# A list schedule that also counts the transfers: softcap attention and a bilinear layer on one core

## The chip, the core and the metric

One core of a Trainium2 chip runs the whole kernel. A time is what one execution takes on the device, in microseconds (us). Of the kernel before there are three runs and one execution with a profile.

## The reference

For 4 batches and 12 heads of 448 rows by 64 columns, in fp32:

```
scores = (q @ k.T) / sqrt(64)
scores = cap * tanh(scores / cap)
attn   = softmax(scores)
x      = attn @ v                        # 1792 x 768 after the heads are put side by side
out    = ((x @ w_a) * (x @ w_b)) @ w_out # 768 -> 1536 -> 768
```

The three weights arrive as float64, so each weight tile is twice as large in DRAM as the fp32 tile that is made of it.

## The kernel before, in words

Attention works on 24 pairs of heads. The first 12 pairs (two batches) are worked through alone. Then the bilinear layer for these two batches (group 0) is interleaved with the attention of pairs 12 to 23, and the layer for group 1 ends the program. TensorE's order is written out by hand (`chain`), and it stays as it is.

A pair goes so. K and Q come in transposed blocks by transfers of their own (`load_k`, four for K and four for Q, two pairs at a time in pairs 2 to 11), and VectorE transposes them (`turn`, tk and tq). TensorE makes the scores of four key blocks (psc), ScalarE takes tanh and exp (pf), VectorE adds up for the row sums (psum), TensorE multiplies with V (`attend`, tile pv, L308) and gathers the sums (L329). Then comes the division: `recip` on VectorE (rec), `store_rec` to DRAM (rd), `load_den` back as a broadcast (den), `scale` on VectorE (L358), and `split_x` into a high and a low part (xhi, xlo). In pairs 0 to 10 the pv bank is `pi % 4`, and pair 11 has bank 0: so the attend of pair 4 waits for the scale of pair 0, and that of pair 11 for the scale of pair 8.

A weight comes in 36 tiles ("units": a0, b0, a1, b1, ... of w_a and w_b, then those of w_out). A raw unit (w64, two transfers of 384 KB, `load64`) is turned into fp32 in six steps on ScalarE, VectorE and GpSimd (`conv`), and then split in two (wha and wla, ...). In group 0 the raw units of the first six come over GpSimd's queue, which also brings V of pairs 3 to 11 (`load_v`); nearly all the other transfers are issued by SyncE (SP). Each queue issues in order, and one that waits holds up all behind it.

Every piece of work is a `job` with an engine, a guessed duration, a lag and what it needs. Due times are worked out backwards from the hand-written chain; then a list schedule walks forward in a modelled time and gives each engine, of the jobs that are ready, the one that is due first. In that model a transfer has only a fixed lag (the last numbers of `job`), however many others are under way. The first four raw units may start from a modelled time of `RAW + 4.0 * (2 * t + n)` on.

Of the kernel before, what the change touches and what calls it, by code (L numbers as in the profile page):

```python
# [119 lines left out]
def kernel(  # L120
# [12 lines left out]
    B, H, S, D = q.shape  # L133
    NT, DM = out.shape
    DFF = w_a.shape[1]
    P = 128
    NP = H // 2
    NK = DM // P
# [57 lines left out]
    own, krem = (slice(0, D), slice(D, P)), (S - R, 0)  # L196
    raw, stk, prob, pvs = {}, {}, {}, {}
# [184 lines left out]
    seq = [(nm, f, g) for g in range(NG) for nm, f in one]  # L382
    wraw, wfull, wspl = {}, {}, {}

    def load64(t, n):
        nm, f, _ = seq[t]
        w = {"a": w_a, "b": w_b, "o": w_out}[nm].bitcast(I32)
        if n == 0:
            wraw[t] = wp.tile([P, DM, 2], I32, tag="w64", name=f"w64{nm}_{f}", bufs=2)
        rt = wraw[t]  # L390
        eng = nc.gpsimd if t < 6 else nc.sync
        if nm == "o":
            eng.dma_start(rt[own[n]].rearrange("p n t -> p (n t)"), w[f * P + n * D : f * P + (n + 1) * D, :])
        else:
            eng.dma_start(
                rt[own[n]].rearrange("p (k f) t -> p k (f t)", k=NK),
                w.rearrange("(j k p) f -> j p k f", j=2, p=D)[n][:, :, 2 * f * P : 2 * (f + 1) * P],
            )

    def conv(t, step):  # L400
# [118 lines left out]
    def job(key, eng, us, fn, args, needs=(), lag=None, after=0.0):  # L519
        jobs[key] = Piece(eng, us, LAG[eng] if lag is None else lag, list(needs), fn, args, after)  # L520
# [133 lines left out]

    used = {"n": 0}
    CYCLE, turns_of = ((0, 1, 2), (3, 1, 2, 0)), [3, 3, 1, 2, None]
    SOON, RAW = 4.0, 18.0
    HASTY = (gate, keep_a, collect, recip, store_rec, load_den, scale)
    GAP = 20.4

# [39 lines left out]
    for r in range(NPG):  # L700
        h = r // NP
        free = [(kind, pi, hf) for kind in ("attend", "add") for pi in (NPAIR - 2, NPAIR - 1) for hf in range(2)]
# [6 lines left out]
    ring = {"o": [], "ab": []}  # L709
    for t, (nm, f, g) in enumerate(seq):  # L710
        if g == 0:
            for n in range(2):
                needs = [("raw", t, 0)] if n else [("conv", t - 2, 5)]
                job(("raw", t, n), "POOL" if t < 6 else "SP", 0.8 if t < 6 else 0.5, load64, (t, n), needs, 6.0, RAW + 4.0 * (2 * t + n) if t < 4 else 0.0)
                jobs["raw", t, n].order_only = n > 0
            steps = (("ACT", 0.82), ("ACT", 0.8), ("DVE", 0.48), ("DVE", 0.48), ("DVE", 0.88), ("POOL", 2.1))
            for n, (eng, us) in enumerate(steps):
                needs = [("raw", t, 0), ("raw", t, 1)] if n == 0 else [("conv", t, n - 1)]
                if n == 1:
                    needs += [("lo", t - AHEAD), ("keepw", t - AHEAD), ("full", t - 1)]  # L720
                job(("conv", t, n), eng, us, conv, (t, n), needs, 2.0 if t < 5 else 0.5)
            job(("keepw", t), "SP", 0.52, store_w, (t,), [("conv", t, 5)], 3.0)
            jobs["full", t] = jobs["conv", t, 1]
            made = ("conv", t, 5)
        else:
            job(("full", t), "SP", 0.5, reload_w, (t,), [("lo", t - AHEAD), ("keepw", t - AHEAD), ("full", t - 1), ("keepw", t - NW)])
            made = ("full", t)
        before = ring["o" if nm == "o" else "ab"]
        free = [("hi", before[-1])] if before else []
        if len(before) >= 3:  # L730
            free.append(used[seq[before[-3]]])
        before.append(t)
        on_dve = g and nm == "b"
        job(("hi", t), "DVE" if on_dve else "ACT", 0.5 if on_dve else 0.74, split_hi, (t,), [made, *free])
        job(("lo", t), "DVE", 0.88, split_lo, (t,), [("hi", t)])
        jobs["w", nm, g, f] = jobs["lo", t]
# [63 lines left out]
    free = dict.fromkeys(LAG, 0.0)  # L800
    line = [jobs[k] for k in chain]
    wait = {e: [] for e in LAG}
    for x in real:
        x.left = len(x.from_)
        x.ready = x.after
        if not x.left and x.eng != "PE":
            wait[x.eng].append(x)
    order, port = [], 0.0
    for x in real:
        x.shared = x.eng == "DVE" and x.fn not in (turn, recip, scale, collect) and not (x.fn is gate and x.args[3] == 0)  # L810
    while len(order) < len(real):
        best = None
        for e, xs_ in wait.items():
            if e == "PE":
                xs_ = line[:1] if line and not line[0].left else []
            if xs_:
                t = max(free[e], min(max(x.ready, port if x.shared else 0.0) for x in xs_))
                if best is None or t < best[0]:
                    best = (t, e, xs_)
        t, e, xs_ = best  # L820
        x = min((x for x in xs_ if max(x.ready, port if x.shared else 0.0) <= t), key=lambda x: x.due - (SOON if x.fn in HASTY else 0.0))
        (line if e == "PE" else wait[e]).remove(x)
        x.start, x.end = t, t + x.us + x.lag
        free[e] = t + x.us
        if x.fn is conv and e == "POOL":
            port = t + x.us
        order.append(x)
        for y in x.then:
            y.left -= 1
            y.ready = max(y.ready, t + x.us if y.order_only and y.eng == x.eng else x.end - y.early.get(id(x), 0.0))  # L830
            if not y.left and y.eng != "PE":
                wait[y.eng].append(y)
# [45 lines left out]
```

## Time and profile before

| | us |
|---|---|
| three runs | 732.89, 737.08, 737.47; median 737.08 |
| the profiled execution | 735.1 |
| its span (first to last instruction) | 733.2 |
| TensorE busy in the span | 706.3 (96%) |
| VectorE, ScalarE, GpSimd busy | 420.9, 349.8, 105.0 |
| mean granted TensorE clock | 0.99 |

The profiled execution is 1.9 us longer than its span. TensorE is the engine that is nearly always busy; the others have long pauses. A row's number in brackets at its end is the idle time of the engine ahead of that instruction and what released it. SPq is SyncE's queue of transfers: there the duration of a row is how long the issue took.

### The profile page before, as it was taken

Reading aid. Unit: us, or ns where it says so; the run is one execution under the profiler, and the core shown is the slowest. Engines: PE = TensorE matmul, PEld = TensorE weight load, DVE = VectorE, ACT = ScalarE, POOL = GpSimd, SP = SyncE. Lnnn points to the kernel's source line nnn. Section 1 sums busy time; section 2 is a strip of 40 time slices with the busy share of each in tenths; the row PEclk is TensorE's granted clock in tenths of the full one; section 3 lists DMA queues with packets and bytes.
Section 4 is the critical chain, followed back from the end, with each engine's and each line's share of the span. In section 5 each row is a group of like instructions: output and inputs, shape, how many; then the busy total and the mean of one; then the engine's idle time right before and its main releaser. Section 6 shows DMA issues by size and latency. Waiting matters only on the chain.

```text
span 733.2 us, 11184 instructions
## 1 busy us (share of the span) xinstructions
PE 706.3 (96%) x4370; PEld 578.8 (79%) x4370; DVE 420.9 (57%) x649; ACT 349.8 (48%) x474; POOL 105.0 (14%) x88
## 2 busy tenths in 40 slices
PE   7868999899999999999999999999999999999996
PEld 2323336598898798798798798999999999999996
DVE  3447996766747868777896847543033434343322
ACT  6875996476776774586655640122322102202100
POOL 0514541122222222222222200000000000000000
PEclk9988999999999999999999999999999999999999
DMA  9988456677777576666575536431022103101012
GB/s 129 185 121 171 128 142 151 151 181 165 168 210 158 139 206 154 148 177 173 149 186 145 156 112 216 155 108 47 19 69 83 43 22 108 44 22 44 1 44 110
DMA packets 142482, 90.54 MB, mean 123 GB/s; under 512 B 107768, under 2 KB 128280, under 8 KB 142424
## 3 DMA queue, kind: packets, MB, share of 16 engines
q1 hardware_dynamic: 135784, 82.53, 45.3%
q0 software_dynamic: 2784, 6.79, 4.0%
q10 hardware_dynamic: 3856, 0.46, 0.5%
q8 instruction: 36, 0.59, 0.4%
q14 instruction: 22, 0.18, 0.1%
HBM read 67.24 MB, written 22.50 MB: 122 GB/s over the span
## 4 chain that ended last, share of the span: by engine, by line
PE 84%; DMA 5%; SPq 4%; DVE 3%; issue 1%; ACT 1%; ACTq 0%; DVEq 0%
PE po L491 8%; PE phb L458 8%; PE po L493 8%; PE po L492 8%; PE phb L460 8%; PE phb L459 8%; PE pha L458 8%; PE pha L460 8%; PE pha L459 8%; PE pv L308 7%; PE psc L271 4%; SPq L220 3%; DMA acc<-in_q_dram 2%; DMA rd<-rec 2%; PE pv L329 1%
## 5 line engine op out<-in xcount | busy, mean ns | idle before, releaser
L491 PE MATMUL po<-who,gh 128*128 128x384 f32 x336 | 113.3, 337 | 0.0
L493 PE MATMUL po<-who,gl 128*128 128x384 f32 x336 | 112.3, 334 | 0.0
L492 PE MATMUL po<-wlo,gh 128*128 128x384 f32 x336 | 112.3, 334 | 0.0
L458 PE MATMUL pha<-xhi,wha 128*128 128x448 f32 x288 | 104.8, 364 | 3.3 <-DVE xhi L374 3.3
L458 PE MATMUL phb<-xhi,whb 128*128 128x448 f32 x288 | 105.1, 365 | 0.0
L460 PE MATMUL pha<-xhi,wla 128*128 128x448 f32 x288 | 104.8, 364 | 0.0
L459 PE MATMUL pha<-xlo,wha 128*128 128x448 f32 x288 | 104.5, 363 | 0.2 <-DVE xlo L375 0.2
L460 PE MATMUL phb<-xhi,wlb 128*128 128x448 f32 x288 | 104.5, 363 | 0.0
L459 PE MATMUL phb<-xlo,whb 128*128 128x448 f32 x288 | 104.2, 362 | 0.0
L283 ACT ACTIVATE pf<-psc,capt 128x896 f32<-128x896 f32 (+1 forms) x96 | 84.4, 910 | 38.9 <-PE psc L271 20.6
L308 PE MATMUL pv<-pf,vb 128*64 128x448 f32 x384 | 80.8, 564 | 8.9 <-DVE den L358 7.1
L287 ACT ACTIVATE pf<-pf,capt 128x1792 f32<-128x1792 f32 (+1 forms) x48 | 77.0, 1605 | 0.7
L502 DVE TENSOR_TENSOR acc<-po,acc 128x384 f32<-128x384 f32 x84 | 46.3, 554 | 44.8 <-PE po L493 44.7
L308 PEld LDWEIGHTS pv<-pf,vb 128*64 128x64 f32 x384 | 26.5, 142 | 56.5 <-issue 38.5
L465 ACT COPY asb<-pha 128x448 f32<-128x448 f32 x48 | 25.6, 533 | 94.0 <-PE pha L460 93.7
L475 DVE TENSOR_TENSOR asb<-phb,asb 128x448 f32<-128x448 f32 x48 | 29.9, 624 | 65.8 <-PE phb L460 65.6
L491 PEld LDWEIGHTS po<-who,gh 128*128 128x128 f32 x336 | 63.1, 188 | 2.7 <-issue 1.5
L492 PEld LDWEIGHTS po<-wlo,gh 128*128 128x128 f32 x336 | 63.1, 188 | 0.1
L493 PEld LDWEIGHTS po<-who,gl 128*128 128x128 f32 x336 | 63.1, 188 | 0.0
L458 PEld LDWEIGHTS pha<-xhi,wha 128*128 128x128 f32 x288 | 53.9, 187 | 9.4 <-DVE xhi L374 3.6
L477 ACT CAST gh<-asb 128x448 fp32r<-128x448 f32 x48 | 27.2, 567 | 67.3 <-DVE asb L475 66.9
L458 PEld LDWEIGHTS phb<-xhi,whb 128*128 128x128 f32 x288 | 53.9, 187 | 6.5 <-issue 2.5
(103 smaller groups left out, 1030.9 us busy)
## 6 DMA issues: line engine op xcount, KB each, us to landing
w64o<-in_moe_w_out_dram SPq DMA_DIRECT2D x24, 384.0 KB
w64a<-in_moe_w_a_dram SPq DMA_DIRECT2D x18, 384.0 KB
w64b<-in_moe_w_b_dram SPq DMA_DIRECT2D x18, 384.0 KB
den<-rd SPq DMA_DIRECT2D x48, 112.0 KB
out_dram<-acc SPq DMA_DIRECT2D x13, 384.0 KB
wda<-wta SPq DMA_DIRECT2D x12, 384.0 KB
wdb<-wtb SPq DMA_DIRECT2D x12, 384.0 KB
wdo<-wto SPq DMA_DIRECT2D x12, 384.0 KB
```

What stands on the lines that cost most here:

```text
L271: nc.tensor.matmul(psc[:, j, :S], kk, tq[y][o], start=(x + y == 0), stop=(x == 1))
L283: nc.scalar.activation(to, prob.pop((pi, "s", c))[:, :n, :S], AF.Tanh, scale=capt[:, 1:2])
L287: nc.scalar.activation(pf, pf, AF.Exp, scale=capt[:, 0:1])
L308: nc.tensor.matmul(t[o, :S], tv[:, j * (NC3 + 1) + (c if j == 0 else (c + 1) % (NC3 + 1))], p, start=(c == 0), stop=(c == NC3))
L458: nc.tensor.matmul(t[:, :S], wh[:, kk], xhi[:, kk, cs], start=(kk == 0), stop=False)
L459: nc.tensor.matmul(t[:, :S], wh[:, kk], xlo[:, kk, cs], start=False, stop=False)
L460: nc.tensor.matmul(t[:, :S], wl[:, kk], xhi[:, kk, cs], start=False, stop=(kk == NK - 1))
L475: nc.vector.tensor_mul(t, phs.pop(("b", h))[:, :S], t)
L491: nc.tensor.matmul(t[:, :HALF], gh[:, cs], wh, start=(f == fs[0]), stop=False)
L492: nc.tensor.matmul(t[:, :HALF], gh[:, cs], wl, start=False, stop=False)
L493: nc.tensor.matmul(t[:, :HALF], gl[:, cs], wh, start=False, stop=(f == fs[-1]))
L502: nc.vector.tensor_add(acc[:, ti, hs], t, acc[:, ti, hs])
```

## The change

The model gets a server for transfers. `MOVE` gives each transfer a duration; `moved` is the time at which the server will have done all that was issued; a transfer that is not `store_rec` or `load_den` may not be issued while more than `BACKLOG` = 3 us are outstanding, and its end is reckoned from the server. `RAW` goes from 18 to 24, the first four raw units come in six transfers each of 128 KB (`parts`), with other earliest times, and the lag behind the conversion steps of the first units is 0.5 where it was 2.0. No arithmetic changes. The order of TensorE's instructions is the same as before; those of the other engines move.

```diff
-    def load64(t, n):
+    def load64(t, n, parts):
...
-        rt = wraw[t]
+        j, i = n % 2, n // 2
+        rt = wraw[t][own[j]]
...
+            ks = slice(2 * i * NK // parts, 2 * (i + 1) * NK // parts)
             eng.dma_start(
-                rt[own[n]].rearrange("p (k f) t -> p k (f t)", k=NK),
-                w.rearrange("(j k p) f -> j p k f", j=2, p=D)[n][:, :, 2 * f * P : 2 * (f + 1) * P],
+                rt.rearrange("p (k f) t -> p k (f t)", k=NK)[:, ks],
+                w.rearrange("(j k p) f -> j p k f", j=2, p=D)[j][:, ks, 2 * f * P : 2 * (f + 1) * P],
             )
...
-    SOON, RAW = 4.0, 18.0
+    SOON, RAW, BACKLOG = 4.0, 24.0, 3.0
...
-            for n in range(2):
-                needs = [("raw", t, 0)] if n else [("conv", t - 2, 5)]
-                job(("raw", t, n), "POOL" if t < 6 else "SP", 0.8 if t < 6 else 0.5, load64, (t, n), needs, 6.0, RAW + 4.0 * (2 * t + n) if t < 4 else 0.0)
+            parts = 6 if t < 4 else 2
+            for n in range(parts):
+                needs = [("raw", t, n - 1)] if n else [("conv", t - 2, 5)]
+                job(("raw", t, n), "POOL" if t < 6 else "SP", 0.8 if t < 6 else 0.5, load64, (t, n, parts), needs, 4.0, RAW + 6.0 * (t + n / parts) if t < 4 else 0.0)
...
-                job(("conv", t, n), eng, us, conv, (t, n), needs, 2.0 if t < 5 else 0.5)
+                job(("conv", t, n), eng, us, conv, (t, n), needs, 0.5)
...
-    order, port = [], 0.0
+    order, port, moved = [], 0.0, 0.0
+    MOVE = {load_k: 0.46, load_v: 0.5, load64: 1.7, store_rec: 0.15, load_den: 0.4, store_w: 1.0, reload_w: 1.0, store_x: 0.57, reload_x: 0.65, store_out: 1.0}
+    def starts(x):
+        t = x.ready
+        if x.shared:
+            t = max(t, port)
+        if x.move and x.fn not in (store_rec, load_den):
+            t = max(t, moved - BACKLOG)
+        return t
...
-                t = max(free[e], min(max(x.ready, port if x.shared else 0.0) for x in xs_))
+                t = max(free[e], min(starts(x) for x in xs_))
...
+        if x.move:
+            moved = max(moved, t + 1.3) + x.move
+            x.end = max(x.end, moved + 0.7)
```

GpSimd's queue in the first 12 pairs, before. vb_175, vb_176 and vb_177 are the three buffers of V; the first two rows bring V of pair 3, which may start once the attend of pair 0 is done, and so on.

```order
L230 DMA vb_175<-in_v_dram 128x3x64 x2
L232 DMA vb_175<-in_v_dram 64x64 x2
L395 DMA w64a_337<-in_moe_w_a_dram 64x6x256 x2
L230 DMA vb_176<-in_v_dram 128x3x64 x2
L232 DMA vb_176<-in_v_dram 64x64 x2
L395 DMA w64b_405<-in_moe_w_b_dram 64x6x256 x2
L230 DMA vb_177<-in_v_dram 128x3x64 x2
L232 DMA vb_177<-in_v_dram 64x64 x2
```

The same queue in the changed kernel:

```order
L230 DMA vb_175<-in_v_dram 128x3x64 x2
L232 DMA vb_175<-in_v_dram 64x64 x2
L230 DMA vb_176<-in_v_dram 128x3x64 x2
L232 DMA vb_176<-in_v_dram 64x64 x2
L397 DMA w64a_402<-in_moe_w_a_dram 64x2x256 x2
L230 DMA vb_177<-in_v_dram 128x3x64 x2
L232 DMA vb_177<-in_v_dram 64x64 x2
L397 DMA w64a_402<-in_moe_w_a_dram 64x2x256 x2
```

Ahead of V of pair 5 (the first vb_177) stood two whole raw units, 1,536 KB; now two pieces of one, 256 KB. The second unit starts four loads of V later.

SP's queue around the first reciprocals, before. rec_403 are those of pair 0, rd_93 is where they go in DRAM, den_433 what comes back.

```order
L220 DMA acc<-in_k_dram 32x28x32
L220 DMA acc<-in_q_dram 32x28x32
L341 DMA rd_93<-rec_403 7x2x64
L351 DMA den_433<-rd_93 64x448 x2
L220 DMA acc<-in_k_dram 32x28x32 x2
L220 DMA acc<-in_q_dram 32x28x32
L341 DMA rd_94<-rec_470 7x2x64
```

The same place in the changed kernel (rec_378 is the former rec_403):

```order
L220 DMA acc<-in_k_dram 32x28x32
L858 TENSOR_LOAD bounded
L858 ISA x2
L341 DMA rd_93<-rec_378 7x2x64
L220 DMA acc<-in_q_dram 32x28x32
L220 DMA acc<-in_k_dram 32x28x32
L220 DMA acc<-in_q_dram 32x28x32
L351 DMA den_418<-rd_93 64x448 x2
L220 DMA acc<-in_k_dram 32x28x32
L341 DMA rd_94<-rec_451 7x2x64
```

The store of pair 0's reciprocals is passed by 14 loads of K and Q that stood ahead of it. Loads now stand between it and the reading back.

SP's queue around the reciprocals of pair 11 (rd_104), before:

```order
L220 DMA ldk_1207<-in_k_dram 32x14x32
L220 DMA ldq_1218<-in_q_dram 32x14x32
L220 DMA ldk_1207<-in_k_dram 32x14x32
L220 DMA ldq_1218<-in_q_dram 32x14x32
L220 DMA ldk_1207<-in_k_dram 32x14x32
L341 DMA rd_104<-rec_1230 7x2x64
L220 DMA ldq_1218<-in_q_dram 32x14x32
L220 DMA ldk_1207<-in_k_dram 32x14x32
L220 DMA ldq_1218<-in_q_dram 32x14x32
L230 DMA vb_177<-in_v_dram 128x3x64 x2
L232 DMA vb_177<-in_v_dram 64x64
L351 DMA den_1286<-rd_104 64x448 x2
```

The same place in the changed kernel:

```order
L220 DMA ldk_1217<-in_k_dram 32x14x32
L220 DMA ldq_1229<-in_q_dram 32x14x32
L341 DMA rd_104<-rec_1219 7x2x64
L220 DMA ldk_1217<-in_k_dram 32x14x32
L220 DMA ldq_1229<-in_q_dram 32x14x32
L220 DMA ldk_1217<-in_k_dram 32x14x32
L220 DMA ldq_1229<-in_q_dram 32x14x32
L220 DMA ldk_1217<-in_k_dram 32x14x32
L220 DMA ldq_1229<-in_q_dram 32x14x32
L351 DMA den_1272<-rd_104 64x448 x2
```

Two loads of pair 14 stand ahead of the store, where five stood; six loads stand between it and the reading back, where three loads and three transfers of V stood.

## Rows read from the trace of the kernel before

**Rows 1.** Busy time by stretches: us, then each engine, granted clock, transfer share, GB/s.

```profile
7.30:35.00 27.70, 25.33 (x168) 8.70 (x168) 11.29 (x22) 26.49 (x27) 10.55 (x16) 1.00 1.09 167
35.00:64.00 29.00, 18.34 (x142) 6.61 (x145) 14.91 (x22) 15.48 (x16) 7.24 (x10) 0.82 0.93 136
64.00:110.70 46.70, 46.68 (x491) 18.34 (x481) 43.89 (x72) 45.13 (x45) 22.89 (x27) 1.00 0.54 144
110.70:144.00 33.30, 28.00 (x206) 19.32 (x199) 23.23 (x41) 17.88 (x29) 3.74 (x2) 0.95 0.64 149
144.00:727.90 583.90, 583.26 (x3379) 523.65 (x3379) 324.73 (x478) 244.41 (x360) 60.41 (x30) 1.00 0.44 118
```

**Rows 2.** Timeline of TensorE, 27 to 143 us: start, us, instruction, idle before.

```profile
27.27 1.77 PE L266 MATMUL psc<-tq,tk 64*128 64x448 f32 x8
...
38.59 2.81 PE L266 MATMUL psc<-tq,tk 64*128 64x448 f32 x8 [3.95 <-DVE tq L237]
41.32 3.84 PE L308 MATMUL pv<-pf,vb 128*64 128x448 f32 x16
...
56.96 4.55 PE L308 MATMUL pv<-pf,vb 128*64 128x448 f32 x16 [7.08 <-DVE den L358]
...
116.48 3.23 PE L308 MATMUL pv<-pf,vb 128*64 128x448 f32 x16 [1.83 <-ACT asb L465]
...
137.23 0.47 PE L458 MATMUL pha<-xhi,wha 128*128 128x448 f32 x1 [3.28 <-DVE xhi L374]
...
138.71 4.64 PE L308 MATMUL pv<-pf,vb 128*64 128x448 f32 x16
```

**Rows 3.** Timeline of SP's queue, 50 to 54 us.

```profile
50.45 0.93 SPq L341 DMA_DIRECT2D rd<-rec  x1
52.73 1.13 SPq L351 DMA_DIRECT2D den<-rd  x2
```

**Rows 4.** Timeline of VectorE, 37 to 57 us.

```profile
37.79 0.65 DVE L237 STREAM_TRANSPOSE tq<-acc 128x448 f32<-128x448 f32 x1 [1.77 <-DMA acc<-in_q_dram]
38.36 0.52 DVE L337 RECIPROCAL rec<-pv 112x64 f32<-112x64 f32 x1
...
56.28 0.62 DVE L358 TENSOR_TENSOR den<-pv,den 128x448 f32<-128x448 f32 x1 [9.46 <-DMA den<-rd]
```

**Rows 5.** Timeline of GpSimd, which issues the raw units.

```profile
20.05 1.34 POOL L395 DMA_DIRECT2D w64a<-in_moe_w_a_dram  x2
```

**Rows 6.** Issues of transfers: size of one, and median us from issue to landing.

```profile
w64a<-in_moe_w_a_dram POOLq DMA_DIRECT2D x6, 384.0 KB, 6.7
vb<-in_v_dram POOLq DMA_DIRECT2D x18, 96.0 KB, 4.2
```

**Rows 7.** Timeline of VectorE, 103 to 136 us: reciprocals and scale of pairs 8 and 11.

```profile
103.42 0.55 DVE L337 RECIPROCAL rec<-rec 112x64 f32<-112x64 f32 x1
...
115.75 0.62 DVE L358 TENSOR_TENSOR den<-pv,den 128x448 f32<-128x448 f32 x1 [1.18 <-DMA den<-rd]
...
122.63 0.55 DVE L337 RECIPROCAL rec<-rec 112x64 f32<-112x64 f32 x1
...
135.71 0.62 DVE L358 TENSOR_TENSOR den<-pv,den 128x448 f32<-128x448 f32 x1 [0.95 <-DMA den<-rd]
```

**Rows 8.** Timeline of SP's queue, 108 to 133 us: the transfers between these.

```profile
108.54 0.80 SPq L341 DMA_DIRECT2D rd<-rec  x1
...
128.25 0.80 SPq L341 DMA_DIRECT2D rd<-rec  x1
129.09 0.43 SPq L220 DMA_DIRECT2D ldq<-in_q_dram  x1
...
132.32 1.18 SPq L351 DMA_DIRECT2D den<-rd  x2
```

**Rows 9.** Waits, 140 to 727 us: who waited for whom, total, times, longest.

```profile
ACT asb L465 <- PE pha L460: 93.7, 38, 4.2
ACT w64o L404 <- DMA w64o<-in_moe_w_out_dram: 14.7, 7, 7.6
```

More of the change, by code (lines that the diff above doesn't have):

```diff
@@ L389, in load64 @@
             wraw[t] = wp.tile([P, DM, 2], I32, tag="w64", name=f"w64{nm}_{f}", bufs=2)
-        rt = wraw[t]
+        j, i = n % 2, n // 2
+        rt = wraw[t][own[j]]
         eng = nc.gpsimd if t < 6 else nc.sync
         if nm == "o":
-            eng.dma_start(rt[own[n]].rearrange("p n t -> p (n t)"), w[f * P + n * D : f * P + (n + 1) * D, :])
+            eng.dma_start(rt.rearrange("p n t -> p (n t)"), w[f * P + j * D : f * P + (j + 1) * D, :])
         else:
+            ks = slice(2 * i * NK // parts, 2 * (i + 1) * NK // parts)
             eng.dma_start(
-                rt[own[n]].rearrange("p (k f) t -> p k (f t)", k=NK),
-                w.rearrange("(j k p) f -> j p k f", j=2, p=D)[n][:, :, 2 * f * P : 2 * (f + 1) * P],
+                rt.rearrange("p (k f) t -> p k (f t)", k=NK)[:, ks],
+                w.rearrange("(j k p) f -> j p k f", j=2, p=D)[j][:, ks, 2 * f * P : 2 * (f + 1) * P],
             )
@@ L717 @@
             for n, (eng, us) in enumerate(steps):
-                needs = [("raw", t, 0), ("raw", t, 1)] if n == 0 else [("conv", t, n - 1)]
+                needs = [("raw", t, i) for i in range(parts)] if n == 0 else [("conv", t, n - 1)]
                 if n == 1:
                     needs += [("lo", t - AHEAD), ("keepw", t - AHEAD), ("full", t - 1)]
-                job(("conv", t, n), eng, us, conv, (t, n), needs, 2.0 if t < 5 else 0.5)
+                job(("conv", t, n), eng, us, conv, (t, n), needs, 0.5)
             job(("keepw", t), "SP", 0.52, store_w, (t,), [("conv", t, 5)], 3.0)
@@ L807 @@
             wait[x.eng].append(x)
-    order, port = [], 0.0
+    order, port, moved = [], 0.0, 0.0
[7 more added lines that the diff above has]
+        return t
     for x in real:
+        x.move = MOVE.get(x.fn, 0.0) * (x.args[3] if x.fn is load_k else 0.2 if x.fn is load_v and x.args[1] > 1 else 2 / x.args[2] if x.fn is load64 else 1.0)
         x.shared = x.eng == "DVE" and x.fn not in (turn, recip, scale, collect) and not (x.fn is gate and x.args[3] == 0)
@@ L820 @@
         t, e, xs_ = best
-        x = min((x for x in xs_ if max(x.ready, port if x.shared else 0.0) <= t), key=lambda x: x.due - (SOON if x.fn in HASTY else 0.0))
+        x = min((x for x in xs_ if starts(x) <= t), key=lambda x: x.due - (SOON if x.fn in HASTY else 0.0))
         (line if e == "PE" else wait[e]).remove(x)
         x.start, x.end = t, t + x.us + x.lag
+        if x.move:
+            moved = max(moved, t + 1.3) + x.move
+            x.end = max(x.end, moved + 0.7)
         free[e] = t + x.us
```

## Prediction

> **What bounds the kernel now.** First the busy time by stretches [rows 1]. From 144 us to 727.9 us TensorE is busy 583.26 of 583.90 us at full clock: no order of the other engines gains anything there. The same holds from 64 to 110.7 us (46.68 of 46.70). What can be had lies in three places: 7.3 to 35 us (25.33 of 27.70 busy), 35 to 64 us (18.34 of 29.00, and the clock only 0.82) and 110.7 to 144 us (28.00 of 33.30). Then TensorE's timeline for the single gaps [rows 2]: 3.95 us ahead of the scores of pair 4, 7.08 us ahead of the attend of pair 4, 1.83 us ahead of that of pair 11, and 3.28 us inside the first product that needs x of pair 11. After the large gaps the same instructions take longer: two score blocks 2.81 us at 38.59 where they took 1.77 at 27.27, an attend 3.84, 4.55 and 4.64 us where it takes 3.23. Then the queues and VectorE for what ended each gap. The sums below are made against the profiled execution, 735.1 us (span 733.2 and 1.9 around it); the median of the three runs is 2.0 higher.
>
> **The gap of 3.95 us.** VectorE transposes Q of pair 4 at 37.79, when that Q lands [rows 4]. From 20.05 us on GpSimd issued two raw units among the loads of K and Q [rows 5], four transfers of 384 KB [rows 6]: 1.57 MB, at the 136 to 167 GB/s of these stretches [rows 1] 9.4 to 11.5 us of transfer time. In the new order GpSimd issues two pieces there, 0.26 MB, so 7.8 to 9.6 us leave the place where 3.95 are missing. Part of the second unit landed behind the Q; if only the first unit counted (0.79 less 0.26 MB, at 167 GB/s 3.1 us), 0.8 us of the gap would stay. I take 3.95, with 3.1 as the lower bound.
>
> **The gap of 7.08 us.** The attend of pair 4 needs the bank of pair 0, so the scale of pair 0, and that came at 56.28 after VectorE had stood idle 9.46 us for den. Its reciprocals were done at 38.88 [rows 4], but SP stored them only at 50.45, because 14 loads of K and Q stood ahead. From the store to the reading back it took 2.28 us, from there to the scale 3.55 [rows 3, 4]. In the new order the store has passed the 14 loads, and the three loads now between it and the reading back fit into the 2.28 us (a load's issue is 0.43 us, [rows 8]). Even with the reciprocals as late as before, the scale would come at 38.9 + 0.5 + 2.3 + 3.6 = 45.3 us. TensorE would ask for it at 56.96 - 7.08 = 49.88, less what the first gap and the slow work behind it give back (3.95 + 1.04 + 0.61 = 5.6), so at 44.3. In that worst case 1 us stays; but the reciprocals now also stand ahead of the transposes of pair 4 on VectorE, one of which ended at 38.44, so they need not be that late. I take 7.08, with 6.0 as the lower bound.
>
> **The slow work behind the two gaps** is 2.81 - 1.77 = 1.04, 3.84 - 3.23 = 0.61 and 4.55 - 3.23 = 1.32, 2.97 us in all. It goes with the gaps: the clock granted was 1.00 until 35 us and 0.82 in the stretch that holds them, between the two levels of 1.2 and 2.4 GHz. The bound from below is 0.61, what follows the smaller gap, should that one alone vanish. First place in sum: 3.95 + 7.08 + 2.97 = **14.0 us**.
>
> **64 to 110.7 us.** Here TensorE has nothing to give, but VectorE (43.89 of 46.70) and ScalarE (45.13) are nearly full. The change takes work out: of the units that were converted here the fourth goes behind the end of the stretch. Nothing, either way. The pieces cost GpSimd more issues: a transfer of a raw unit is 0.67 us of its time [rows 5], four more for each of four units are 10.7 us, of an engine with 22.89 of 46.70 us busy here and 7.24 of 29.00 before that [rows 1]. Behind them wait V and the last conversion step, both with several us to spare. I cost this at nothing.
>
> **The gap of 1.83 us.** The row names ScalarE, but the attend of pair 11 needs bank 0, the scale of pair 8, which ran from 115.75 to 116.37, released by den [rows 7]; TensorE went on at 116.48. The reciprocals were there at 103.97, the store went out at 108.54 [rows 8], again late in SP's order. In the new order it still stands behind a load of V that waits for an attend, and six loads follow before the reading back. So 0 to 1.83 us; I take the middle, 0.9.
>
> **The gap of 3.28 us.** x of pair 11 is late: reciprocals done at 123.18, stored at 128.25, read back from 132.32, scale at 135.71 [rows 7, 8]. The new order has two loads ahead of the store where five stood, and six issues between store and reading back as before. Three issues of 0.43 are 1.3 us, the lower bound; the upper is the gap. I take 2.0, since the 5.1 us between reciprocal and store hold more than these three. The attend behind it took 4.64 us, 1.41 over 3.23. After the 1.83 us gap the attend took 3.23, so behind a gap of 1.3 us the slow work should be gone too: 1.41, from below 0. Together 3.4.
>
> **Sum.** 14.0 + 0.9 + 3.4 = 18.3 us, so 716.8 against the profiled 735.1. The median of before is 2.0 above the profiled run; the waits for loads are what may differ between runs, and most of them go, so I add half: **718 us**. With all upper values (20.5) it would be 714.6, with the lower ones (3.1 + 6.0 + 2.97 + 0 + 1.3 + 0 = 13.4) 721.7, and up to 2 more by the median: 714 to 724.
>
> **A rule that speaks against the pieces.** A raw transfer of 384 KB lands 6.7 us after its issue, one of 96 KB on the same queue 4.2 [rows 6]: the time hardly follows the size. By a straight line between them a piece of 128 KB takes 4.5 us (an estimate). If pieces ran one behind the other, a unit would take 27 us where two transfers took 13.4, 13.6 more; since issues are 0.67 us apart and each lands us later, they overlap, and I charge nothing. The Trainium skill, DMA: Bandwidth & Descriptors, section Anatomy of one DMA — SWDGE (gpsimd) path, puts a fixed cost of some 2.0 us on each transfer of this queue; taken one after the other, four more per unit would be 8 us, an estimate, and the sum 724.8 if one unit lay bare. The trace agrees that small ones are dear (4.2 us for 96 KB), and does not show them in a row.
>
> **Rivals.**
> - *The Q of pair 4 stays late* (13%). The server of the model is not the chip: the rows put 167 GB/s on a stretch with many small transfers, and Q could be held up by those and not by the raw units. Then 3.95 + 1.04 + 0.61 stay: 716.8 + 5.6 = 722.4. Against it: 1.57 MB are much for 10 us.
> - *The weights take over the wait* (13%). The conversions start later by about a unit; at the start of the bilinear layer a low part could come late on VectorE, already full. Then the 4.3 us of the last two gaps are not gained, and a new wait like that of pair 11 appears, 3.28 + 1.41 = 4.7: 14.0 - 4.7 = 9.3, so 725.8. For it: VectorE 94% busy ahead of that place. Against it: the first two units are still converted before.
> - *Slower: ScalarE stands behind raw units in the long stretch* (5%). SP's later order changes too; loads of K and Q stand in larger blocks ahead of the raw units of w_out. ScalarE takes its work in order, and a wait for a raw unit holds up the copies that free TensorE's banks. Seven such waits cost 14.7 us, the longest 7.6, and reached TensorE nowhere, because ScalarE had waits for TensorE of up to 4.2 us to spend [rows 9]. If all 12 units of w_out waited 7.6 us, 12 x (7.6 - 4.2) = 41 us would come on top: 758. It decides once each waits 1.5 us beyond the slack (18.3 / 12).
> - *The pieces run one behind the other* (4%), by the straight line above: 13.6 us once on the path, 730.4.
> - *It does not do what it says* (3%): the order moves, but the chip's transfers end when they did: 735.
>
> That leaves 62% for the forecast. The range of **713 to 727** holds the forecast and the first two rivals with the runs' scatter. About 1% (7 us) can be told from no change: faster by more than 1% is 84% (forecast and first two rivals, less 4% at the upper edge), within 1% 11%, slower 5%.
>
> **What would show it.** Right: in TensorE's timeline no gap over 1 us between the scores of pair 4 and the attend of pair 5, attends of 3.2 us throughout, the full stretch of attention over at about 96.7 us where it ended at 110.7 [rows 1], and the first bilinear product there; in SP's queue the first store of reciprocals a few us behind the reciprocal. Wrong: a transpose of Q still released by its load behind TensorE's need; or the first product early, and then waits for a low part of a weight; or TensorE idle after 144 us.

## The result and the profile after

| us | before | changed |
|---|---|---|
| median of the runs (lowest to highest) | 737.28 (732.89 to 738.52) | 717.75 (716.13 to 718.51) |
| profiled execution | 735.1 | 718.51 |
| TensorE busy in the span | 706.3 (96%) | 703.4 (98%) |

The ratio is 0.9743, 95% interval 0.9699 to 0.9786; the forecast was 718.0. In the profiled executions the gain is 16.6 us. That is the figure that the rows can be held against, since the profiled execution of before lies in the lower half of its runs and that of the change is the highest of its four.

Busy time by stretches of the changed kernel, in the columns of [rows 1], cut where the same work begins and ends:

```profile
7.30:35.00 27.70, 25.57 (x170) 9.01 (x172) 17.09 (x31) 25.89 (x25) 9.60 (x15) 1.00 1.14 150
35.00:64.00 29.00, 29.00 (x266) 10.83 (x262) 21.61 (x35) 26.26 (x25) 12.85 (x21) 1.00 1.08 166
64.00:96.70 32.70, 32.61 (x349) 12.80 (x350) 29.07 (x46) 31.66 (x33) 18.82 (x27) 1.00 0.64 157
96.70:110.70 14.00, 14.00 (x133) 10.29 (x125) 13.03 (x24) 11.38 (x17) 4.72 (x4) 1.00 0.80 196
110.70:144.00 33.30, 30.43 (x174) 23.54 (x175) 22.48 (x36) 19.73 (x30) 7.02 (x6) 0.95 0.69 164
144.00:711.40 567.40, 566.77 (x3293) 509.44 (x3291) 316.86 (x466) 232.60 (x349) 58.74 (x30) 1.00 0.43 118
```

From 35 to 64 us TensorE now never stops and has its full clock; it had 18.34 busy us of 29 at a clock of 0.82. What stood at 110.7 us stands at 96.7. One stretch with something left remains, 110.7 to 144 us.

TensorE's timeline answers to [rows 2]: the scores and the attend of pair 4, the attend of pair 11, the product with x of pair 11 and the attend behind it.

```profile
34.69 1.77 PE L266 MATMUL psc<-tq,tk 64*128 64x448 f32 x8
...
44.04 3.23 PE L308 MATMUL pv<-pf,vb 128*64 128x448 f32 x16
...
100.79 3.23 PE L308 MATMUL pv<-pf,vb 128*64 128x448 f32 x16
...
120.96 0.47 PE L460 MATMUL pha<-xhi,wha 128*128 128x448 f32 x1 [2.68 <-DVE xhi L374]
...
122.52 4.55 PE L308 MATMUL pv<-pf,vb 128*64 128x448 f32 x16
```

Three of the four gaps have no bracket any more. The attend of pair 11 comes 15.69 us earlier (116.48 to 100.79), nearly the whole gain. The fourth gap went from 3.28 to 2.68, and the attend behind it from 4.64 to 4.55.

SP's queue and VectorE at the first reciprocals, against [rows 3, 4]:

```profile
28.11 0.92 SPq L341 DMA_DIRECT2D rd<-rec  x1
29.09 0.38 SPq L220 DMA_DIRECT2D acc<-in_q_dram  x1
29.52 0.64 SPq L220 DMA_DIRECT2D acc<-in_k_dram  x1
30.21 1.51 SPq L220 DMA_DIRECT2D acc<-in_q_dram  x1
34.31 1.14 SPq L351 DMA_DIRECT2D den<-rd  x2
```

```profile
27.53 0.56 DVE L337 RECIPROCAL rec<-pv 112x64 f32<-112x64 f32 x1 [1.98 <-PE pv L329]
...
30.87 0.65 DVE L237 STREAM_TRANSPOSE tq<-acc 128x448 f32<-128x448 f32 x1
...
38.53 0.62 DVE L358 TENSOR_TENSOR den<-pv,den 128x448 f32<-128x448 f32 x1 [0.54 <-DMA den<-rd]
```

The store has passed the 14 loads and goes out 0.6 us after the reciprocal begins, where it waited 12 us. The reading back then comes 6.20 us behind the store, not 2.28. This costs nothing here: the scale ends at 39.15 and the attend of pair 4 asks at 44.04. Q of pair 4 is transposed at 30.87, 3.8 us before its scores.

SP's queue around the reciprocals of pair 11, GpSimd's raw unit b2 at the same place, and the scale on VectorE, against [rows 7, 8]:

```profile
108.39 0.80 SPq L341 DMA_DIRECT2D rd<-rec  x1
109.24 0.42 SPq L220 DMA_DIRECT2D ldk<-in_k_dram  x1
...
111.79 0.48 SPq L220 DMA_DIRECT2D ldq<-in_q_dram  x1
112.37 1.12 SPq L351 DMA_DIRECT2D den<-rd  x2
```

```profile
111.36 1.31 POOL L397 DMA_DIRECT2D w64b<-in_moe_w_b_dram  x2 [0.30 <-POOL wtb L420]
```

```profile
105.61 0.55 DVE L337 RECIPROCAL rec<-rec 112x64 f32<-112x64 f32 x1
...
118.97 0.62 DVE L358 TENSOR_TENSOR den<-pv,den 128x448 f32<-128x448 f32 x1 [3.06 <-DMA den<-rd]
```

The store came 2.2 us after its reciprocal where it came 5.1 after it. But from the issue of the reading back to the scale it now takes 6.60 us, where it took 3.39 (132.32 to 135.71): what the store won, the reading back lost. The reading back now goes out 1.0 us behind b2; in the kernel before, b2 had been issued at 108.80, 23.5 us ahead of it. That the gap is 0.60 us shorter all the same comes from VectorE, whose reciprocals were done 1.34 us after TensorE's sums, where it had been 2.67.

### The profile page after: what moved, and what is told of

It is laid out like the page before. It is cut to its first block, busy times and chain, and to the rows that moved or that the text cites. A ratio compares the mean times of both kernels' runs of the same rounds, so it can differ in the third digit from the quotient of the medians.

```text
span 716.7 us, 11238 instructions
## 1 busy us (share of the span) xinstructions
PE 703.4 (98%) x4370; PEld 578.3 (81%) x4370; DVE 423.0 (59%) x649; ACT 347.7 (49%) x474; POOL 112.0 (16%) x104
## 4 chain that ended last, share of the span: by engine, by line
PE 92%; DMA 3%; SPq 2%; DVE 1%; ACT 1%; issue 0%; ACTq 0%; DVEq 0%
PE pv L308 10%; PE po L493 8%; PE po L494 8%; PE po L495 8%; PE phb L460 8%; PE phb L462 8%; PE phb L461 8%; PE pha L460 8%; PE pha L462 8%; PE pha L461 8%; PE psc L266 5%; PE psc L271 3%; DMA den<-rd 2%; PE pv L329 2%; SPq L220 1%; PE psc L274 1%
## 5 line engine op out<-in xcount | busy, mean ns | idle before, releaser
L308 PE MATMUL pv<-pf,vb 128*64 128x448 f32 x384 | 78.8, 553 | 0.0
```

The source lines that it names most:

```text
L308: nc.tensor.matmul(t[o, :S], tv[:, j * (NC3 + 1) + (c if j == 0 else (c + 1) % (NC3 + 1))], p, start=(c == 0), stop=(c == NC3))
```

## The experiments

All times are medians; a ratio is to the kernel before on the same chip.

**1. Only later raw units** (kernel before):

```diff
-    SOON, RAW = 4.0, 18.0
+    SOON, RAW = 4.0, 40.0
```

> The kernel before with one number changed: the raw units may start from a modelled 40 us on, where 18 stood. SyncE's order up to the first store of reciprocals stays as it was (14 loads ahead of it); GpSimd brings V of pairs 3 to 6 ahead of the first unit. Theory (the 3.95 us gap is raw units among the loads of K and Q of pair 4, the 7.08 us gap is the store of reciprocals behind 14 loads): the 3.95 us and the 1.65 us of slow work behind them go, the second gap stays at 5 to 7 us, in all 5 to 8 us faster than before, 728 to 732 us. Rival (one cause: the transfers that the raw units crowd out; the store is late only because the 14 loads ahead of it are): both gaps go, 12 to 14 us faster, 723 to 726 us. Rival (Q of pair 4 is held up by many small transfers): the first gap stays, same time as before.

738.16 us, ratio 1.0029 (1.0004 to 1.0053): nothing gained. Its SP queue, then TensorE:

```profile
41.74 0.93 SPq L341 DMA_DIRECT2D rd<-rec  x1
49.09 1.13 SPq L351 DMA_DIRECT2D den<-rd  x2
```

```profile
53.31 4.71 PE L308 MATMUL pv<-pf,vb 128*64 128x448 f32 x16 [9.10 <-DVE den L358]
...
274.42 0.44 PE L491 MATMUL po<-who,gh 128*128 128x384 f32 x1 [2.14 <-DVE acc L502]
```

The first gap is gone: Q of pair 4 is transposed at 29.60. So raw units among the loads made that gap. The second grew to 9.10 us. The store still stands behind the 14 loads, 11.05 us after its reciprocals (30.69), and the first raw unit now goes out around it:

```profile
40.77 0.68 POOL L395 DMA_DIRECT2D w64a<-in_moe_w_a_dram  x1
...
42.51 0.68 POOL L395 DMA_DIRECT2D w64a<-in_moe_w_a_dram  x1
```

The reading back comes 7.35 us behind the store, where it took 2.28. That alone is more than the 2.02 us by which the gap grew. The attend of pair 4 still came 3.65 us earlier and that of pair 11 3.2; this was lost after 200 us, where TensorE was busy 196.27 of 200 us.

**2. Only the server**, with whole raw units at their former times and the former lags:

```diff
-    SOON, RAW, BACKLOG = 4.0, 24.0, 3.0
+    SOON, RAW, BACKLOG = 4.0, 18.0, 3.0
...
-            parts = 6 if t < 4 else 2
+            parts = 2
...
-                job(("raw", t, n), ..., needs, 4.0, RAW + 6.0 * (t + n / parts) if t < 4 else 0.0)
+                job(("raw", t, n), ..., needs, 6.0, RAW + 4.0 * (2 * t + n) if t < 4 else 0.0)
...
-                job(("conv", t, n), eng, us, conv, (t, n), needs, 0.5)
+                job(("conv", t, n), eng, us, conv, (t, n), needs, 2.0 if t < 5 else 0.5)
```

> The change without its pieces: the server of transfers and its bound stay, the raw units come in two transfers each, from a modelled 18 us on with the old spacing and lags. The first raw unit (786 KB) again goes out ahead of V of pair 4; the store of pair 0's reciprocals stands 17 issues earlier than before. Theory: the 7.08 us gap is gone; of the 3.95 us gap up to 0.8 us stays; in all 17 to 19 us faster than before, within 2 us of the whole change. Rival (the pieces carry the gain of the first gap): 3.95 + 1.65 us stay, 5 to 6 us slower than the whole change.

723.25 us, ratio 0.9827 (0.9783 to 0.9872): two thirds of the gain. The 7.08 us are gone, since the store stands ahead; the gap ahead of the scores of pair 4 is 2.07 (3.95 before), that ahead of the attend of pair 11 is 1.61, that of the product 3.15. The time is the rival's (5 to 6 us above the change), but of the first gap only half stayed.

**3. Raw units at once** (the change, with no earliest time for the first four):

```diff
-..., needs, 4.0, RAW + 6.0 * (t + n / parts) if t < 4 else 0.0)
+..., needs, 4.0, 0.0)
```

> The whole change, but the raw units in pieces may start at once (no earliest time): two units, 1.57 MB, go out at the very start, beside K and Q of pairs 0 to 3, and are through before Q of pair 4 is issued; the third follows from the first conversion on. The store of reciprocals stands early as in the change. Theory (what matters is which loads the raw bytes stand among): 1.57 MB at 150 to 167 GB/s are 9 to 10 us; the waits move to pairs 1 to 4, 6 to 12 us slower than the whole change, 724 to 730 us. Rival (only the place of the store of reciprocals matters): same as the change, 717 to 719 us.

735.08 us, ratio 0.9994 (0.997 to 1.0018). It was worse than either theory had it. GpSimd, then TensorE:

```profile
4.96 2.37 POOL L397 DMA_DIRECT2D w64b<-in_moe_w_b_dram  x4
```

```profile
18.25 4.11 PE L266 MATMUL psc<-tq,tk 64*128 64x448 f32 x12 [11.26 <-DVE tk L237]
```

The raw bytes now stand ahead of K and Q of the first pairs, and TensorE waits 11.26 us for them. When the raw bytes come is worth as much as the whole change.

**4. The change with two transfers for a unit**, planned so:

```diff
-            parts = 6 if t < 4 else 2
+            parts = 2
```

> The whole change with the raw units in two transfers each (384 KB) where six stood; earliest times and the server unchanged. Theory (the pieces are neither dear nor needed, only the order counts): within 2 us of the whole change, 716 to 720 us. Rival (a transfer of 384 KB holds up the loads of K and Q as one lump, which pieces avoid): a gap of 1 to 4 us ahead of pair 4 or 5, 719 to 723 us. Rival (pieces are dear, each pays a fixed price): 1 to 3 us faster than the change.

728.99 us, ratio 0.9906 (0.9874 to 0.9937), 11 us above the change: the theory that the pieces cost or bring nothing fell. Gaps of 0.99, 1.10, 2.21, 1.03 and 3.45 us came back between 82 and 128 us. Of this kernel GpSimd's raw unit and SP's queue behind it:

```profile
57.51 1.34 POOL L397 DMA_DIRECT2D w64a<-in_moe_w_a_dram  x2
```

```profile
59.88 0.87 SPq L341 DMA_DIRECT2D rd<-rec  x1
67.29 1.83 SPq L351 DMA_DIRECT2D den<-rd  x2
```

and the same place in the changed kernel:

```profile
57.01 1.20 POOL L397 DMA_DIRECT2D w64b<-in_moe_w_b_dram  x2
```

```profile
59.32 0.80 SPq L341 DMA_DIRECT2D rd<-rec  x1
...
64.04 1.11 SPq L351 DMA_DIRECT2D den<-rd  x2
```

Ahead of the store GpSimd has issued 768 KB here and 256 KB there; the store is readable after 7.41 and after 4.72 us. SP waits in its queue, and K and Q of pairs 10 and 11 stand behind: a transpose waits 7.05 us for K at 80.19. But this kernel's whole order differs, so experiment 9 takes the size alone.

**5. No bound** (the change):

```diff
-    SOON, RAW, BACKLOG = 4.0, 24.0, 3.0
+    SOON, RAW, BACKLOG = 4.0, 24.0, 1000.0
```

> The whole change with the bound set so high that it never acts (BACKLOG 1000 where 3 stood): pieces, earliest times and the server's reckoning of ends stay, a load may be issued however much is outstanding. SyncE's order then again has 14 loads ahead of the first store of reciprocals. Theory (the bound alone moves the store; without it a gap ahead of the attend of pair 4 stays, as large as with the raw units sent later alone): a gap of 6 to 10 us there, 9 to 14 us slower than the whole change, 727 to 733 us. Rival (the server's ends and the pieces carry the gain): 717 to 721 us.

745.53 us, ratio 1.0141 (1.0103 to 1.0179): slower than before, and some 27 us above the change where 9 to 14 were expected. SP's queue, then TensorE:

```profile
49.71 0.93 SPq L341 DMA_DIRECT2D rd<-rec  x1
...
56.57 1.15 SPq L351 DMA_DIRECT2D den<-rd  x2
```

```profile
62.34 4.65 PE L308 MATMUL pv<-pf,vb 128*64 128x448 f32 x16 [18.20 <-DVE den L358]
```

The reciprocals were done at 28.11, and the store again stands behind the 14 loads. The bound is what moves it: without it the planner hands all loads to SP as soon as they are ready.

**6. The reading back of pair 11 first** (the change, with the loads of K and Q between store and reading back put behind it):

```diff
+    held = [jobs["den", NPG - 1, j] for j in range(2)]
+    lo_, hi_ = order.index(jobs["rd", NPG - 1]), order.index(held[1])
+    late_ = [x for x in order[lo_:hi_] if x.fn is load_k]
+    order = [x for x in order if not any(x is y for y in late_)]
+    at_ = order.index(held[1]) + 1
+    order[at_:at_] = late_
```

> The whole change with one thing moved: on SyncE's queue the reading back of pair 11's reciprocals goes ahead of the six loads of pair 14 that stood between it and its store. Theory (the 2.7 us gap inside the product that needs x of pair 11 is left because the reading back is issued 2 us late, and then beside 768 KB of raw unit and the loads; from 108 to 112 us the transfer engines moved only 64 GB/s): read back at about 110.5 us where 112.4 stood, scale at about 116 us where 118.97 stood, gap under 0.7 us and the attend behind it 3.2 us where 4.55 stood; 3 to 4 us faster than the change, 713.5 to 715 us. Rival (the store lands late whatever follows it): the gap stays, 717 to 718.5 us. Rival (the six loads are missed by the next pair): a new gap at the scores of pair 14, same time as the change or slower.

715.67 us, ratio 0.9726 (0.9699 to 0.9752). SP's queue, then TensorE:

```profile
108.64 0.80 SPq L341 DMA_DIRECT2D rd<-rec  x1
110.53 1.12 SPq L351 DMA_DIRECT2D den<-rd  x2
```

```profile
119.09 3.23 PE L308 MATMUL pv<-pf,vb 128*64 128x448 f32 x16
...
171.22 0.44 PE L493 MATMUL po<-who,gh 128*128 128x384 f32 x1 [1.45 <-ACT acc L502]
```

The last gap is gone, and the slow attend with it. But this edit does two things. The reading back is issued 1.89 us behind its store, not 3.98; and it now goes ahead of the raw unit b2 (issued at 111.39), behind which it stood in the change. Which of the two held pair 11 this run alone doesn't say. 1.45 us come back at 171 us, where ScalarE has waited 4.05 us for a raw unit (168.02) ahead of the copy that frees a bank.

**7. The raw unit b2 later** (the change; b2 is the one that GpSimd issues at that place):

```diff
+                if (t, n) == (5, 0):
+                    needs.append(("scale", NPG - 1))
```

> The whole change with one need more: the sixth raw unit (768 KB) may start only after the scale of pair 11. SyncE's order stays. Theory (what makes the reading back take 6.6 us to the scale, where it took 3.4 before the change, is the raw unit issued 1 us ahead of it): scale at 116 to 117 us, gap 0 to 1 us, 2 to 4 us faster than the change, 714 to 716 us. Rival (the six loads of K and Q and those of V are what it stands behind): gap stays over 2 us, same time. Rival: the unit itself comes late and ScalarE waits for it, 1 to 3 us lost later.

718.96 us, ratio 0.9772 (0.9744 to 0.9799). The edit did not move the raw unit: a need binds only the planner's model, no wait on the chip follows from it, and the orders of GpSimd and SP came out as in the change. GpSimd, then SP's queue:

```profile
111.21 1.31 POOL L397 DMA_DIRECT2D w64b<-in_moe_w_b_dram  x2 [0.30 <-POOL wtb L420]
```

```profile
111.45 1.12 SPq L351 DMA_DIRECT2D den<-rd  x2
```

The reading back still stands just behind b2; the scale comes at 118.89 after a wait of 3.07, and TensorE waits 2.71 us. So this run is the change once more, and neither its theory nor its rivals were put to the test.

**8. Half the bound** (the change):

```diff
-    SOON, RAW, BACKLOG = 4.0, 24.0, 3.0
+    SOON, RAW, BACKLOG = 4.0, 24.0, 1.5
```

> The whole change with BACKLOG 1.5 where 3 stood. SyncE's order has the store of pair 11's reciprocals ahead of all loads of pair 14, and two of them before the reading back, where six stood. Theory (small transfers are served sooner when less is outstanding): from store to reading back of pair 0 4 to 5 us where 6.2 stood; the last gap shrinks by 1 to 3 us; 1 to 4 us faster than the change, 713.5 to 717 us. Rival (with so little outstanding the loads of K and Q come too late): a gap of 1 us or more ahead of the scores of pairs 4 to 11, 719 to 725 us.

715.83 us, ratio 0.9729 (0.9698 to 0.9761). SP now has two loads between the store and the reading back of pair 11 instead of six (and four transfers of V), and b2 goes out at 114.23, 2.85 us behind the reading back. TensorE:

```profile
119.68 0.48 PE L460 MATMUL pha<-xhi,wha 128*128 128x448 f32 x1 [1.30 <-DVE xhi L374]
...
120.94 3.23 PE L308 MATMUL pv<-pf,vb 128*64 128x448 f32 x16
```

The scale of pair 11 (117.70) no longer waits for den. It stands behind VectorE's own work, in which one cast took 1.81 us, where casts of this size take some 0.4 to 0.8; what is left of the gap is VectorE's.

The next four ran on one chip.

**9. Whole raw units at the changed order's places** (each transfer of 384 KB where the second of its three pieces stood; nothing else moves):

```diff
         j, i = n % 2, n // 2
+        if parts == 6:
+            if i != 1:
+                return
+            i, parts = 0, 2
```

> The changed kernel with every instruction in its changed order, except that the first four raw units come in two transfers of 384 KB, each at the place of the second of its three pieces. Theory (large transfers hold up small stores and loads that stand behind them; this is what cost the kernel with two transfers 11 us): some store of reciprocals is read back 7 us or more after its issue, gaps of 1 to 3 us come back between 75 and 110 us, 721 to 727 us. Rival (those 11 us came from the order that the list schedule then made, in which a store stood late, and not from the size of a transfer): within 1 us of the change, 716.5 to 719 us, and no gap over 0.5 us ahead of 110 us.

723.2 us, ratio 0.9828 (0.9804 to 0.9852), 4.4 us above the change on this chip (experiment 12). So in this order the size of the pieces is worth 4.4 us, and the rest of experiment 4 was its order. The place was not the one expected: no gap over 0.4 us ahead of 110 us. SP's queue, then TensorE:

```profile
93.61 3.96 SPq L351 DMA_DIRECT2D den<-rd  x2
...
99.82 1.66 SPq L341 DMA_DIRECT2D rd<-rec  x2
...
106.62 2.86 SPq L351 DMA_DIRECT2D den<-rd  x4
```

```profile
124.38 0.74 PE L464 MATMUL pha<-xhi,wha 128*128 128x448 f32 x1 [5.84 <-DVE xhi L374]
```

In the change the store of pairs 9 and 10 went out at 98.36, just ahead of a raw unit of 768 KB (99.24), and was read back at 101.14, 2.78 us later. Here an issue of 3.96 us (1.13 in the change) made it 1.5 us late, behind that unit (98.88), and it took 6.80 us. Pair 11 stands behind it. Why that one issue took longer stays open. The whole units did not hold up the stores as a rule: from store to reading back, pairs 0 to 7 together take 32.1 us here and 31.9 in experiment 12.

**10. Only the bound**, the ends of transfers by their fixed lag:

```diff
-            x.end = max(x.end, moved + 0.7)
```

> The changed kernel with the bound on what is outstanding, but the end of a transfer reckoned by its fixed lag as before. Theory (the bound alone moves the stores ahead of the loads, the new ends do nothing): 716.5 to 719.5 us, no gap ahead of the attend of pair 4. Rival (the new ends carry a part too): later loads are planned too early, gaps of 1 us or more ahead of scores come back, 721 us or more.

724.98 us, ratio 0.9853 (0.983 to 0.9877), 6.2 above the change. The time is the one that the rival gave, the place is one that neither gave: up to the product of pair 11 (120.99 us) it stands as the change does. Two losses show: the attend behind that product takes 5.50 us (4.25 in experiment 12), and between 200 and 400 us TensorE is busy 197.01 of 200 us, its gaps released by VectorE, while ScalarE waits up to 7.3 us for raw units. Of the 5.5 us between the spans these are 4.2, and the gap itself is 0.54 shorter (2.75 against 3.29), so 1.8 stay open. What the reckoned ends are worth shows mostly in the long stretch.

**11. Half the bound and the reading back first:** the edits of 6 and 8 together.

> The changed kernel with half the bound (1.5 us) and the reading back of pair 11 ahead of the loads that stood between. If the two gains add up (each about 2 us by itself; the gap of 1.30 us at 119.68 us goes): 713.5 to 715.0 us. If what one saves is lost again behind, as 1.45 us at 171 us with the reading back alone: 715.2 to 716.2 us, and the windows show it between 144 and 200 us.

716.7 us, ratio 0.9733 (0.9709 to 0.9758), 2.1 below the change beside it. The two gains don't add up, nor is 144 to 200 us the place (56.00 of 56.00 busy):

```profile
119.45 0.47 PE L460 MATMUL pha<-xhi,wha 128*128 128x448 f32 x1 [1.18 <-DVE xhi L374]
...
120.72 4.92 PE L308 MATMUL pv<-pf,vb 128*64 128x448 f32 x16
```

Both edits bring the reading back ahead of b2 (109.62 against 114.00 here), so there was only one gain to have. The scale (117.47) again stands behind VectorE's own work, with a cast of 1.80 us. And here the attend ran slow, at a clock of 0.64 from 120 to 124 us.

**12. The change again.**

> The changed kernel itself, run beside the three others of this call on one chip: 717 to 719 us, with the gap of 2.7 us ahead of the product of pair 11, the slow attend behind it, and no other gap over 1 us between 20 and 711 us. If it comes out below 716.5 us, the gains of about 2 us of the earlier variants were the chip's and not theirs.

718.82 us, ratio 0.9764 (0.9739 to 0.9789), with a gap of 3.29 us ahead of the product and an attend of 4.25 us behind it.

**What held the reading back of pair 11.** No run moves b2 alone, but the traces can be laid side by side. The fourth column is the time from the issue of the reading back to the scale, the last how long VectorE stood idle for den ahead of that scale (where it didn't, the fourth column holds other work of VectorE):

| run | b2 issued | reading back issued | to the scale | idle for den |
|---|---|---|---|---|
| before | 108.80 | 132.32 | 3.39 | 0.95 |
| 4 | 105.20 | 121.71 | 3.73 | 1.43 |
| the change | 111.36 | 112.37 | 6.60 | 3.06 |
| 12 | 111.17 | 111.30 | 8.01 | 3.65 |
| 7 | 111.21 | 111.45 | 7.44 | 3.07 |
| 10 | 111.43 | 111.61 | 7.39 | 3.01 |
| 9 | 114.06 | 115.99 | 6.41 | 3.94 |
| 6 | 111.39 | 110.53 | 5.32 | 0 |
| 8 | 114.23 | 111.38 | 6.32 | 0 |
| 11 | 114.00 | 109.62 | 7.85 | 0 |

In before and in experiments 4, 7, 8, 9, 10 and 12 six transfers stand between the store and the reading back, as in the change, and den is late in some of them and not in others: the transfers on SP's queue don't sort them. The place of b2 does. With b2 issued 0.1 to 1.9 us ahead, it is 6.4 us or more to the scale and VectorE waits 3 us or more; with b2 long through, 3.4 to 3.7 us; with b2 behind, VectorE does not wait for den. And in experiment 12 the reading back went out 1.1 us earlier than in the change, without gain. Of the other runs, in 1 and 2 b2 was through as well (3.42 us to the scale with 0.42 idle, and no idle time for den); in 3 and 5 SP itself issued raw transfers in between (6.09 and 5.39 us, 1.45 and 0.81 idle).

## Why the prediction was right

By its own steps, in the profiled executions:

| step | forecast | measured |
|---|---|---|
| gaps 3.95 and 7.08, slow work 2.97 | 14.0 | 13.9 |
| gap 1.83 | 0.9 | 1.83 |
| gap 3.28 | 2.0 | 0.60 |
| slow attend behind it | 1.41 | 0.09 |
| behind 127 us | 0 | 0.2 |
| sum | 18.3 | 16.6 |

The first row is the 15.69 us by which the attend of pair 11 is earlier, less 1.83.

- *The first gap* was read rightly, and experiment 1 shows its cause: with the raw units away it goes.
- *The second gap* too: experiments 1 and 5, both with the 14 loads ahead of the store, keep it (9.10 and 18.20 us). One number in this step was wrong. The reading back did not follow in 2.28 us but in 6.20. The three loads now between are not why: experiments 3 and 9 have three there too, with no raw piece in flight, and take 2.65 and 3.28 us. With one piece of 128 KB issued just ahead of the store it is 2.65 and 3.63 (8 and 11), with two 5.24 to 6.20 (the change, 6, 7, 10 and 12), with 768 KB 8.07 (4). It was covered by what the step had named without counting on it: the reciprocals came 10.8 us earlier (27.53 against 38.36). In the worst case that the step reckoned with, 4.9 us would have stayed instead of 1.
- *The two gaps stand in a row.* The prediction added them, which holds since both go. Removed alone (experiment 1), the first gave 5.44 us ahead of the second gap, and 3.65 were left behind it; the second had grown by 2.02.
- *The gap of 1.83* went whole: the scale of pair 8 ran at 99.82, ahead of the 100.79 at which TensorE asked. The middle between 0 and 1.83 was taken for want of a row.
- *The gap of 3.28* is the step that failed. The forecast took 2.0 us from the store's wait for SP's issues, and 2.84 came (5.07 to 2.23); it took the reading back to cost what it had, and that leg grew by 3.21 us (3.39 to 6.60). It counted the transfers on SP's queue and left out where GpSimd's b2 would stand: 1.0 us ahead of the reading back, with the transfer engines full (share 1.03 at 216 GB/s from 112 to 116 us). The table above bears this out over ten traces; b2 landed at 117.95, and the scale ran at 118.97. That b2 is the cause is so far read from traces, as experiment 7, which was to move it, didn't.
- *The pieces*, charged at nothing, are worth 4.4 us (experiment 9). The prediction bounded them from above alone; a gain was not among its terms. How they bring it is known only as far as experiment 9 goes, down to one slow issue. Twelve pieces of w_a landed in 3.4 us, twelve of w_b in 4.6, about the estimated 4.5 or under it. They overlap: the six of b1, issued from 89.79 us on, 0.60 us apart, had all landed at 97.37. The Trainium skill's fixed cost of some 2.0 us on each (DMA: Bandwidth & Descriptors, Anatomy of one DMA — SWDGE (gpsimd) path) did not add up here: six times 2.0 would be 12 us, an estimate, and it was 7.6.

```profile
w64a<-in_moe_w_a_dram POOLq DMA_DIRECT2D x12, 128.0 KB, 3.4
w64b<-in_moe_w_b_dram POOLq DMA_DIRECT2D x12, 128.0 KB, 4.6
```

- *The median.* 1 us was added for the scatter; the measured median lies 0.8 below the profiled run. With the sum 1.7 too high the two errors cancel, so 718.0 against 717.75 is closer than the working was: that part is luck. The lower sum took 2.97 for the slow work, where its step had named 0.61 as a bound; with that it is 724.1, still inside the range.
- *The rivals.* Neither a late Q nor a late weight appeared. The slow rival (ScalarE behind raw units in the long stretch) did not occur in the change, where TensorE is busy 566.77 of 567.40 us, but is no fiction: experiment 6 loses 1.45 us that way. Experiments 1 and 10 lose 3.7 and 3.0 us in the same stretch, where the rows name VectorE as what released the gaps and ScalarE had stood behind raw units; that the one made the other isn't shown.

## What to carry to other kernels

A planner that gives each transfer a fixed lag sends every load as soon as it may go, and the few small transfers on the critical path stand behind them; a bound on what is outstanding, from which those few are exempt, changes that (without it the same kernel was slower than before, with half of it faster still). Read such a chain from end to end, store, reading back and use, and count what else is in transfer during each leg, since a leg's length in the old trace holds only for the load it had. Count the other queues too: here it was a large transfer of GpSimd's, issued just ahead, that went with every long leg, and not the loads on SP's own queue. Of two waits in a row, the removal of one can lengthen the other. And look up in the trace whether an experiment moved what it was to move, as an order in the planner is not a wait on the chip.

## What the runs showed of the hardware

A store of 3.5 KB could be read back 1.89 us after its issue with nothing between on its queue (experiment 6), after 2.78 us just ahead of a raw unit (the change), and after 6.80 to 8.07 just behind one (experiments 4 and 9). Between the two rows of experiment 4, 512 KB more cost 2.69 us; at the 167 GB/s of that stretch 512 KB take 3.1. In the changed kernel the first seven stores are read back 0.2 to 1.3 us after the landing of the last raw piece that was issued ahead of them. The Trainium skill (DMA: Bandwidth & Descriptors, Queues, rings and completion order) says that an engine goes round its queues packet by packet, and also that the write that tells of a landing comes only after every earlier write of that engine, on all its queues. By the first the bytes of a small store on SP's queue would pass a large transfer on GpSimd's; by the second its landing would still be told behind that transfer's earlier writes, and these rows agree. The kernels differ in more than that, so this is not isolated.

How slow the attend behind the last gap ran did not follow the gap's length: 3.23 us after 1.30 (experiment 8), 4.92 after 1.18 (experiment 11), 4.55 after 2.68, 4.25 after 3.29, 5.50 after 2.75 (experiment 10). The granted clock from 120 to 124 us was 1.00, 0.64, 0.73, 0.71 and 0.56 in that order: a mean of stretches at 1.2 and at 2.4 GHz. The forecast that a gap of 1.3 us leaves no slow work held in one of these two kernels (8 and 11); attends that came directly behind gaps of 1.03 to 1.83 us took 3.23 us in before and in experiments 1, 2 and 4.
